# Forty short dummy matmuls instead of ten long ones at the head of an attention-and-experts kernel

## The chip, the cores and the metric

The kernel runs on one core of one Trainium2 chip. The metric is the device time of one execution in microseconds. The kernel before takes 563.89 us, the median of three runs (562.78 to 564.74).

TensorE (PE in the profile) multiplies matrices; VectorE (DVE), ScalarE (ACT) and GpSimd (POOL) do the elementwise work; SyncE (SP) issues nearly all DMAs. Each engine takes its instructions in the order in which the program lists them.

## The reference

```python
# sparse causal attention, B, H, S, D = 2, 8, 576, 64
scores = scale * np.matmul(q, k.transpose(0, 1, 3, 2))
mask_local = (rel >= 0) & (rel < 32)                     # heads 0 to 3
mask_strided = (rel >= 0) & (pos_k % 32 == pos_q % 32)   # heads 4 to 7
attn = softmax(np.where(masks, scores, -1e9))
x = np.matmul(attn, v)                                   # tokens 1152 x 512
# first layer, weights in float64
h = np.maximum(np.maximum(x @ w1, x @ w2), x @ w3)       # 512 -> 768
x = h @ w_out                                            # 768 -> 512
# four experts, all of them for every token
p = domain_probs / (domain_probs.sum(-1, keepdims=True) + 1e-09)
for e in range(4):
    out += p[:, e:e+1] * (np.maximum(x @ w1[e], 0) @ w2[e])   # 512 -> 1024 -> 512
```

## The kernel before

The 1152 tokens are worked on in four parts i (two batches, each in halves of 256 and 320 tokens), and the heads in four pairs p. The head of the program issues loads and then ten dummy matmuls: a tile `warm` is set to zero on VectorE (line 219), and line 222 multiplies it with itself into a PSUM bank that nobody reads. Their sole effect is that TensorE is at work while the first inputs are on their way.

Attention of a part and a pair has these steps. `att_a` (lines 280 to 339) puts the mask `mk` into a PSUM tile `sps` by a matmul with the identity (L306), adds the scores by float32 matmuls (L309), takes the maximum of each row on VectorE (L314), subtracts it in one of three ways (L325 on TensorE, L328 on VectorE, or as the bias of the exponential, L318 and L322) and takes the exponential on ScalarE (L322, L331, L334) into `p`. `att_n` divides by the sum: the reciprocal on VectorE (L355), the product on GpSimd (L361). `att_t` transposes `p` on TensorE (`tps`, L373) and ScalarE copies it to SBUF (`pt`, L376). `att_p` multiplies by the values (`ops`, L403); ScalarE and VectorE write the result as a pair of float16 tiles, high and low part, into `x` (L410, L411).

The first layer's weights come as float64 in six pieces `w_0` to `w_5` of 1.5 MB each into two staging buffers `st64_0` and `st64_1`. `decode64` makes float32 of them on VectorE, ScalarE and GpSimd (L198 to L214; the result for all six is one buffer `r`), `scale_w` finds a scale (a pass on ScalarE, L162; then small steps that end in the reciprocal `s`, L136), and `split_w` makes a high and a low float16 part (for `w_0` on GpSimd and ScalarE: L452, L453, L454). `g1` then multiplies `x` by the three matrices with three float16 matmuls for each product (L416 high by high, L417 high by low, L418 low by high). The second layer and the experts follow in the same float16 pairs.

In which order these steps are written is a table of names (`ORDER`). The order in which the instructions of each engine stand in the program is worked out from it when the program is built, by a scheduler that keeps a simulated timeline with costs of its own and, whenever an engine is free in it, takes the foremost step that is ready there. A change of what an early instruction costs in that timeline can thus move instructions far behind it.

Each tile has few buffers, and a later step waits until the earlier one has let go: two PSUM banks for `sps` (three for another tag that the first pairs use as well), two for `tps`, one for `ops`, one buffer for `r`.

Of the kernel before, what the change touches and what calls it, by code (L numbers as in the profile page):

```python
# [8 lines left out]
F32 = mybir.dt.float32  # L9
F16 = mybir.dt.float16  # L10
BF16 = mybir.dt.bfloat16
I32 = mybir.dt.int32
U16 = mybir.dt.uint16
AF = mybir.ActivationFunctionType
ALU = mybir.AluOpType
# [3 lines left out]
B, H, S, D = 2, 8, 576, 64  # L19
NT, DM, DFF = 1152, 512, 768  # L20
E, FE = 4, 1024
QN = (256, 320)

ATT = (((4, 64, 96, 288, 64), (4, 64, 64, 256, 64)), ((5, 64, 96, 352, 64), (6, 60, 108, 648, 108)))
NEG = -8.0e9
NWARM = 10
SUB = 'ddoppdpppoooodod'
ACC = 'bgbbgggggbggbggg'
SGN = 'dddpppdp'
# [30 lines left out]
TW = 'dddddddd'  # L60
TLO = 'd'
WHI = 'aaapaa'
TINY = 2.0**-100
REBIAS = 2.0**-112
TINY64 = 1.625 * 2.0**-124
# [3 lines left out]
def kernel(ctx, tc, qk0l, qk0s, qk1l, qk1s, vl, vs0, vs1, vn, masks, w123, wo, probs, we1, we2, out):  # L69
    nc = tc.nc  # L70
# [5 lines left out]
    x2acc = x2tp.tile([128, 4 * NT], F32, name="x2acc")  # L76
    x2j = [
        x2acc[:, 8 * QN[0] * j : 8 * (QN[0] + QN[1] * j)].rearrange("p (k b t) -> p k b t", k=4, b=2) for j in range(2)
    ]
# [14 lines left out]
    tp = moe_stack.enter_context(tc.tile_pool(name="tp", bufs=3))  # L94
# [21 lines left out]
    def nm(p):  # L116
        uid[0] += 1
        return f"{p}{uid[0]}"
# [20 lines left out]
    def scale_of(maxes, n, inv=None, f=0.25):  # L139

        allr, m = all_max(maxes, n)
        nc.vector.tensor_scalar(m, allr, TINY, f, ALU.max, ALU.mult)
        if inv is None:
# [45 lines left out]
    def decode64(g):  # L189
        hw, lw, r = groups[g]  # L190
        if not f64:
            return

        t = st64[g % 2]
        gi = hw.bitcast(I32)
        if LOW[g] == "a":
            top = t.bitcast(U16).rearrange("p (n t) -> p n t", t=4)[:, :, 1]
            nc.scalar.activation(lw, top, AF.Copy, bias=2.0**-14 - 0.5, scale=2.0**-13)  # L198
        else:
            nc.vector.tensor_scalar(lw, lw, 29, None, ALU.logical_shift_right)  # L200
        if SGN[g] == "d":
            nc.vector.scalar_tensor_tensor(lw, gi, -0x80000000, lw, ALU.bitwise_and, ALU.bitwise_or)
        else:
            sign = t.bitcast(BF16).rearrange("p (n t) -> p n t", t=4)[:, :, 1]
            nc.gpsimd.tensor_scalar(sign, hw, 0.0, 1.0, ALU.mult, ALU.mult)
        if REB[g] == "a":
            nc.scalar.activation(hw, hw, AF.Copy, scale=REBIAS)
        elif REB[g] == "p":
            nc.gpsimd.tensor_scalar(hw, hw, REBIAS, 1.0, ALU.mult, ALU.mult)
        else:  # L210
            nc.vector.tensor_scalar(hw, hw, REBIAS, None, ALU.mult)
        r = rp.tile([128, NP], F32, tag="r", name=nm("r")) if g < NF1 else hw
        gi, ri = hw.bitcast(I32), r.bitcast(I32)
        nc.vector.scalar_tensor_tensor(ri, gi, 3, lw, ALU.logical_shift_left, ALU.bitwise_or)  # L214
        groups[g][2] = r


    warm = tp.tile([128, 320], F32, tag="t1", name="warm")[:, :256].bitcast(BF16)
    nc.vector.memset(warm, 0.0)
    wps = ps.tile([128, 512], F32, tag="mm", name="wps")  # L220
    for _ in range(NWARM):
        nc.tensor.matmul(wps, warm[:, :128], warm, start=True, stop=True)

    tab = const.tile([128, 1], F32, name="tab")
    nc.scalar.activation(tab, warm[:, :1], AF.Exp)
# [2 lines left out]
    identb = const.tile([128, 128], BF16, name="identb")  # L228
# [14 lines left out]

    xs = [xp.tile([128, 4, 2, QN[i % 2]], F16, tag="x", name=f"x{i}") for i in range(4)]
    vinv = [None] * 4
    vsc = [None] * 4
    loaded = {}
# [32 lines left out]
    def att_a(i, p):  # L280
        hf = i % 2
        loc = p < 2
        t = loaded[i, p]
        ng, w, nk, kcols, kstep = ATT[hf][0 if loc else 1]
        rows = 2 * w
# [57 lines left out]
    def att_n(i, p):  # L343
        ng, w, nk, kcols, kstep = ATT[i % 2][0 if p < 2 else 1]
        rows = 2 * w
# [17 lines left out]
    def att_t(i, p):  # L363
        ng, w, nk, kcols, kstep = ATT[i % 2][0 if p < 2 else 1]
        rows = 2 * w
# [15 lines left out]
    def att_p(i, p):  # L381
        hf = i % 2
        loc = p < 2
        ng, w, nk, kcols, kstep = ATT[hf][0 if loc else 1]
        rows = 2 * w
        vt = loaded[i, "v", 0 if loc else 1]
        ov = psa.tile([128, 512], F32, tag="o", bufs=1, name=nm("ops"))
        for c0, n, ptt in pts_of[i, p]:
            for j in range(n):
                g = c0 + j  # L390
                for a in range(2):
                    rhs = ptt[:nk, j * rows + a * w : j * rows + a * w + w]
                    col = 128 * (p % 2) + 64 * a
                    lhsT = vt[:, g, col : col + 64]
                    if loc:
                        o = ov[64 * a : 64 * a + 64, 64 * g : 64 * g + 64]
                    else:
                        nr = (8, 6)[hf]
                        o = ov[64 * a : 64 * a + 64, : w * ng].rearrange("p (m c) -> p m c", c=nr * ng)[
                            :, :, nr * g : nr * g + nr  # L400
                        ]
                        rhs = rhs.rearrange("p (m r) -> p m r", r=nr)
                    nc.tensor.matmul(o, lhsT, rhs, start=True, stop=True)  # L403
        if loc:
            src = ov[:, : 64 * ng]
            dst = [xs[i][:, p, j, :] for j in range(2)]
        else:
            src = ov[:, : w * ng].rearrange("p (m c) -> p m c", c=(8, 6)[hf] * ng)[:, :, :32]
            dst = [xs[i][:, p, j, :].rearrange("p (m r) -> p m r", r=32) for j in range(2)]
        nc.scalar.activation(dst[0], src, AF.Copy, scale=vsc[i])  # L410
        nc.vector.scalar_tensor_tensor(dst[1], src, vsc[i], dst[0], ALU.mult, ALU.subtract)  # L411

    def mm3(psum, pairs):
        n = len(pairs)
# [27 lines left out]
    def split_w(fc):  # L442
        hi, lo = [ws[fc][j].rearrange("p w k f -> p (w k f)") for j in range(2)]
        r = groups[fc][2]
        if WLO[fc] == "d":
            if WHI[fc] == "a":
                nc.scalar.activation(hi, r, AF.Copy, scale=wsc[fc])
# [10 lines left out]
    def g1(i, fc):  # L458
        n = QN[i % 2]
        if fc == 0:  # L460
# [20 lines left out]
    def g2(i, dc):  # L481
        n = QN[i % 2]
        x2 = x2j[i % 2][:, dc, i // 2, :]
# [52 lines left out]
    def x2_ops(j, pool):  # L536
        n = QN[j]
        s, xinv[j] = scale_of(x2mx[:, j::2, :], 8, f=2.0)
# [106 lines left out]
    def gemm1(e, j, fp):  # L645
        ops = wx[e, 1][0]
        n = QN[j]
        hh = hbuf[0] if j else hbuf[1 + e % 2]
# [120 lines left out]
    def first_hidden():  # L769
        if "m" not in gens:  # L770
            open_h0()
            gens["m"] = stream((fp, lambda fp=fp: gemm1(0, 0, fp)) for fp in range(4))
        next(gens["m"])

    ATOMS = {
        "cl": open_rest,
        "m": lambda: first_hidden(),
        "yw": lambda: gen_step("x1", lambda: x2_ops(1, lay["left"])),
        "lq": load_qk, "lv": load_v, "lw": load_w, "lo": load_wo,
# [8 lines left out]
    for a in ORDER.split():  # L788
        name = a.rstrip("0123456789")
# [212 lines left out]
def _layout(inputs):  # L1002
# [102 lines left out]
```

## Time and profile before

| what | value |
|---|---|
| median of three runs | 563.89 us |
| the profiled execution | 563.27 us |
| its span, first to last instruction | 561.5 us |
| TensorE busy | 544.6 us (97%) |
| VectorE, ScalarE, GpSimd busy | 410.6, 345.4, 101.0 us |
| mean granted clock of TensorE | 0.978 |

The span is 1.8 us shorter than the time of the execution it belongs to. Busy time of TensorE says that it had a matmul in flight, not that it ran at its peak. The granted clock is a share of full speed: 1.00 is 2.4 GHz and 0.50 is 1.2 GHz. In the 40 slices of the page the clock is below 0.9 in the first three slices alone, that is in the first 42 us.

### The profile page before, as it was taken

To read this page: it belongs to the slowest core of one execution; us is meant where nothing else is said; L and a number is where in the kernel's file an instruction comes from. 1 tells how busy PE (TensorE), PEld (TensorE's weight loads), DVE (VectorE), ACT (ScalarE), POOL (GpSimd) and SP (SyncE) were. 2 spreads that over 40 slices of the span, in tenths; PEclk is the share of its full clock that TensorE was granted. 3 is DMA by queue.
4 is the path that set the end of the run, shared out by engine and by line. 5 is a ranking of instruction groups with operands and counts; after the bars stand their busy time and mean duration, and the time that the engine had idled before them with its cause. 6 is when DMAs were issued, how large, how long until landed. Compare 5 with 4: busy or idle time off the path is not lost.

```text
span 561.5 us, 11622 instructions
## 1 busy us (share of the span) xinstructions
PE 544.6 (97%) x4681; PEld 450.3 (80%) x4681; DVE 410.6 (73%) x794; ACT 345.4 (62%) x794; POOL 101.0 (18%) x82
## 2 busy tenths in 40 slices
PE   7899999999999999999999999999889999999997
PEld 4678788888877778778888877888767888877886
DVE  3979989662459424779564789898888999878832
ACT  3588676655245255999876877347887544777200
POOL 0465871710112103000000300000130000120000
PEclk7679999999999999999999999999999999999999
DMA  8999633024004000204516001544501321101332
GB/s 311 336 410 277 189 121 114 2 76 152 1 5 148 1 0 1 76 20 152 188 66 198 2 1 40 150 149 142 161 1 39 118 90 57 40 1 31 130 104 75
DMA packets 24150, 58.60 MB, mean 104 GB/s; under 512 B 3272, under 2 KB 3528, under 8 KB 23328
## 3 DMA queue, kind: packets, MB, share of 16 engines
q1 hardware_dynamic: 23952, 57.57, 31.4%
q8 instruction: 36, 0.59, 0.5%
q10 hardware_dynamic: 144, 0.30, 0.1%
q14 instruction: 18, 0.15, 0.1%
HBM read 48.42 MB, written 9.44 MB: 103 GB/s over the span
## 4 chain that ended last, share of the span: by engine, by line
PE 84%; DMA 6%; DVE 4%; ACT 4%; POOL 1%; issue 0%; SPq 0%; DVEq 0%; ACTq 0%
PE e L827 15%; PE w L827 13%; PE g L416 9%; PE g L417 9%; PE g L418 8%; PE e L659 4%; PE e L660 4%; PE e L661 4%; PE w L659 4%; PE w L661 4%; PE w L660 4%; PE ops L403 2%; DMA st<-in_w_dram 2%; PE sps L309 2%; DMA mk<-in_masks_dram 1%; PE tps L373 1%
## 5 line engine op out<-in xcount | busy, mean ns | idle before, releaser
L827 PEld LDWEIGHTS <-hb 128*128 128x128 f16 x1056 | 103.1, 98 | 12.6
L418 PE MATMUL g<-x,w 128*128 128x256 f16 (+1 forms) x288 | 82.0, 287 | 0.0
L417 PE MATMUL g<-x,w 128*128 128x256 f16 (+1 forms) x288 | 82.0, 287 | 0.0
L416 PE MATMUL g<-x,w 128*128 128x256 f16 (+1 forms) x288 | 80.8, 287 | 1.0 <-ACT x L410 0.6
L659 PE MATMUL e<-xops,w1ops 128*128 128x320 f16 (+1 forms) x224 | 63.7, 288 | 2.9 <-ACT c L670 1.5
L660 PE MATMUL e<-xops,w1ops 128*128 128x320 f16 (+1 forms) x224 | 64.2, 288 | 0.0
L659 PE MATMUL w<-xops,w1ops 128*128 128x256 f16 (+1 forms) x224 | 63.4, 284 | 0.8 <-DVE c L687 0.6
L661 PE MATMUL e<-xops,w1ops 128*128 128x320 f16 (+1 forms) x224 | 64.1, 288 | 0.0
L660 PE MATMUL w<-xops,w1ops 128*128 128x256 f16 (+1 forms) x224 | 63.4, 284 | 0.0
L661 PE MATMUL w<-xops,w1ops 128*128 128x256 f16 (+1 forms) x224 | 62.9, 284 | 0.0
L660 PEld LDWEIGHTS <-w1ops 128*128 128x128 f16 x448 | 43.8, 98 | 15.0 <-issue 4.7
L661 PEld LDWEIGHTS <-w1ops 128*128 128x128 f16 x448 | 43.8, 98 | 11.0
L659 PEld LDWEIGHTS <-w1ops 128*128 128x128 f16 x448 | 43.8, 98 | 10.3
L417 PEld LDWEIGHTS <-w 128*128 128x128 f16 x288 | 28.2, 98 | 8.1 <-issue 1.1
L416 PEld LDWEIGHTS <-w 128*128 128x128 f16 x288 | 28.2, 98 | 8.0 <-issue 0.8
L418 PEld LDWEIGHTS <-w 128*128 128x128 f16 x288 | 28.3, 98 | 7.4 <-issue 0.2
L476 POOL TENSOR_TENSOR h<-t,h 128x320 f16<-128x320 f32 (+1 forms) x18 | 16.4, 916 | 88.2 <-ACT h L475 88.2
L162 ACT ACTIVATE junk<-st 128x512 f16<-128x512 f32 x44 | 27.8, 631 | 5.6 <-DMA st<-in_we_dram 4.7
L827 PE MATMUL w<-B,hb 128*128 128x256 f16 x240 | 29.4, 273 | 0.0
L169 ACT ACTIVATE w1ops<-st,s 128x1024 f16<-128x1024 f32 x19 | 21.4, 1144 | 12.9 <-DVE st L584 4.8
L827 PE MATMUL e<-B,hb 128*128 128x256 f16 x240 | 29.1, 273 | 0.0
L714 POOL TENSOR_TENSOR hb<-c,hb 128x512 f16<-128x512 f32 x7 | 9.0, 1279 | 108.7 <-ACT hb L713 99.8
(232 smaller groups left out, 1318.4 us busy)
## 6 DMA issues: line engine op xcount, KB each, us to landing
st<-in_we_dram SPq DMA_DIRECT2D x10, 1024.0 KB, 5.3
st<-in_w_dram SPq DMA_DIRECT2D x6, 1536.0 KB, 9.7
c<-accd SPq DMA_DIRECT2D x24, 256.0 KB, 2.8
accd<-c SPq DMA_DIRECT2D x23, 256.0 KB, 2.3
st<-in_wo_dram SPq DMA_DIRECT2D x2, 1536.0 KB, 6.4
st<-in_we_dram SPq DMA_DIRECT2D x6, 512.0 KB, 4.6
x2acc<-in_we_dram SPq DMA_DIRECT2D x6, 512.0 KB, 4.3
qk<-in_qk1s_dram SPq DMA_DIRECT2D x4, 684.0 KB, 11.8
```

Of the source, the lines that this page charges most:

```text
L162: nc.scalar.activation(junk, src, AF.Abs, scale=2.0**-12, accum_out=dst)
L169: nc.scalar.activation(hi, src, AF.Copy, scale=s)
L309: nc.tensor.matmul(s3[:, j, :], qv[:, g, :], t[:, kstep * g : kstep * g + nk], start=False, stop=j == n - 1)
L403: nc.tensor.matmul(o, lhsT, rhs, start=True, stop=True)
L416: nc.tensor.matmul(psum, lh, rh, start=i == 0, stop=False)
L417: nc.tensor.matmul(psum, lh, rl, start=False, stop=False)
L418: nc.tensor.matmul(psum, ll, rh, start=False, stop=i == n - 1)
L476: eng(HLO[6 * i + fc]).tensor_tensor(hh[:, 1, fc, :], t1[:, :n], hh[:, 0, fc, :], ALU.subtract)
L659: nc.tensor.matmul(pt, wh, xh, start=first and k == 0, stop=False, skip_group_check=True)
L660: nc.tensor.matmul(pt, wh, xl, start=False, stop=False, skip_group_check=True)
L661: nc.tensor.matmul(pt, wl, xh, start=False, stop=k == 1, skip_group_check=True)
L827: nc.tensor.matmul(pt, hop[:, x, f, sl], wop[:, y, f, :], start=start and n == 0, stop=stop and n == 11, skip_group_check=True)
```

## The change

The dummy matmuls are forty of 256 columns instead of ten of 512. Their operand is the head of `x2acc`, a large tile that is written by real work only much later, instead of a tile of its own. Nothing else that the program executes is altered by hand: the matmuls of `att_p` now start a PSUM group at the first block alone (`start=g == 0`), and the remaining lines add options (`XLO`, a value "a" of `SGN`, an atom "z" of `ORDER`) that no table uses here. Line numbers rise by 1 to 4 in `decode64`, by 8 in `att_a` to `att_t` and by 15 in `g1` (L200 becomes L201, L202 L206, L211 L215, L214 L218, L306 L314, L309 L317, L325 L333, L361 L369, L162 L163, L416 L431).

```diff
-NWARM = 10
+NWARM = 40
...
-    warm = tp.tile([128, 320], F32, tag="t1", name="warm")[:, :256].bitcast(BF16)
+    warm = x2acc[:, :128].bitcast(BF16)
     nc.vector.memset(warm, 0.0)
     wps = ps.tile([128, 512], F32, tag="mm", name="wps")
-    for _ in range(NWARM):
-        nc.tensor.matmul(wps, warm[:, :128], warm, start=True, stop=True)
+
+    def keep_warm(n):
+        for _ in range(n):
+            nc.tensor.matmul(wps[:, :256], warm[:, :128], warm, start=True, stop=True)
+
+    keep_warm(NWARM)
...
-                    nc.tensor.matmul(o, lhsT, rhs, start=True, stop=True)
+                    nc.tensor.matmul(o, lhsT, rhs, start=g == 0, stop=True, skip_group_check=True)
```

The scheduler places the instructions of attention and of the first layer's first parts anew on every engine, up to the part of 320 columns; behind that the order is the old one. Numbers in the names below are those of the tiles: `p11` and `p61` are the same tiles before and after, only the last number differs.

On VectorE, about 20 us into the program, `s30` is the scale of the weight piece `w_0`, and `st64_1` the staging buffer of `w_1`. Before:

```order
L131 TENSOR_REDUCE rows42_276<-rows42_276 128x1
L145 TENSOR_SCALAR sinv_134<-rows29_230 128x1
L200 TENSOR_SCALAR st64_1_72<-st64_1_72 128x1536
L142 TENSOR_SCALAR rows42_276<-rows42_276 128x1
L338 TENSOR_REDUCE asm25_210<-p23_208 128x4
L136 RECIPROCAL s30_235<-sinv_134 128x1
L202 SCALAR_TENSOR_TENSOR st64_1_72<-st64_1_72 128x1536
```

Now:

```order
L146 TENSOR_SCALAR sinv_163<-rows29_259 128x1
L132 TENSOR_REDUCE rows42_305<-rows42_305 128x1
L137 RECIPROCAL s30_264<-sinv_163 128x1
L143 TENSOR_SCALAR rows42_305<-rows42_305 128x1
L346 TENSOR_REDUCE asm25_239<-p23_237 128x4
L201 TENSOR_SCALAR st64_1_72<-st64_1_72 128x1536
L146 TENSOR_SCALAR inv43_309<-rows42_305 128x1
```

The scale of `w_0` now stands ahead of the first decoding step of `w_1` (L200 before, L201 now).

On GpSimd, `r27` and `w123_0` are the two steps that split `w_0`; `p35`, `p23` and `p11` are three products of `att_n`. Before:

```order
L452 TENSOR_SCALAR r27_226<-r27_226,s30_235 128x1536
L361 TENSOR_TENSOR p35_253<-p35_253,ar49_296 128x384
L454 TENSOR_TENSOR w123_0_142<-r27_226,w123_0_142 128x1536
L361 TENSOR_TENSOR p23_208<-p23_208,ar56_318 128x256
L361 TENSOR_TENSOR p11_171<-p11_171,ar58_323 128x384
```

Now:

```order
L467 TENSOR_SCALAR r27_255<-r27_255,s30_264 128x1536
L469 TENSOR_TENSOR w123_0_171<-r27_255,w123_0_171 128x1536
L369 TENSOR_TENSOR p35_282<-p35_282,ar49_325 128x384
L369 TENSOR_TENSOR p23_237<-p23_237,ar56_347 128x256
L369 TENSOR_TENSOR p11_200<-p11_200,ar58_352 128x384
```

The low part of `w_0` has moved ahead of `p35`, and `p11` is now the third product behind it, not the second.

On ScalarE, `p61` is an exponential that frees a bank of `sps`, and `w123_1` with `mx89` the pass over the decoded `w_1` (`r34`). Before:

```order
L322 ACTIVATE p61_339,asm63_341<-sps64_342,amx62_340 128x64 x4
L349 ACTIVATE ars72_377<-asm63_341 128x4
L410 ACTIVATE x0_130<-ops112_520,s44_282 128x256
L198 ACTIVATE st64_0_71<-st64_0_71 128x1536
L162 ACTIVATE w123_1_222,mx89_444<-r34_251 128x1536
L376 COPY pt66_359<-tps65_354 96x512
L322 ACTIVATE p75_386,asm77_388<-sps78_389,amx76_387 128x64 x4
```

Now:

```order
L418 ACTIVATE x0_159<-ops112_549,s44_311 128x256
L163 ACTIVATE w123_1_251,mx89_473<-r34_280 128x1536
L330 ACTIVATE p61_368,asm63_370<-sps64_371,amx62_369 128x64 x4
L199 ACTIVATE st64_0_71<-st64_0_71 128x1536
L384 COPY pt66_388<-tps65_383 96x512
L330 ACTIVATE p75_415,asm77_417<-sps78_418,amx76_416 128x64 x4
L384 COPY pt68_395<-tps67_390 64x512
```

The exponential `p61` stood two places ahead of the copy of `x0`; it now stands behind the pass over `w_1`.

On VectorE at the same place, `sps82` and `sps87` are tiles of scores whose maxima are taken, and `st64_0` holds the weight piece `w_2`. Before:

```order
L202 SCALAR_TENSOR_TENSOR st64_0_71<-st64_0_71 128x1536
L314 TENSOR_REDUCE sps82_404<-sps82_404 128x4
L211 TENSOR_SCALAR st64_0_71<-st64_0_71 128x1536
L318 TENSOR_SCALAR amx80_402<-sps82_404 128x4
L314 TENSOR_REDUCE amx85_422<-sps87_424 120x3
```

Now:

```order
L322 TENSOR_REDUCE sps82_433<-sps82_433 128x4
L206 SCALAR_TENSOR_TENSOR st64_0_71<-st64_0_71 128x1536
L326 TENSOR_SCALAR amx80_431<-sps82_433 128x4
L215 TENSOR_SCALAR st64_0_71<-st64_0_71 128x1536
L363 RECIPROCAL ar73_408<-ars72_406 128x4
L322 TENSOR_REDUCE amx85_451<-sps87_453 120x3
```

Two decoding steps of `w_2` (L202 and L211 before, L206 and L215 now) stood on either side of the maximum of `sps82`; both now stand between it and the maximum of `sps87`.

## Rows read from the trace of the kernel before

**Rows 1.** Busy time (instructions) of PE, PEld, DVE, ACT, POOL; granted clock; DMA share, GB/s.
```profile
40.00:60.00 20.00, 20.00 (x193) 17.03 (x192) 18.42 (x40) 16.58 (x65) 12.02 (x8) 1.00 0.79 235
```

**Rows 2.** Timeline, start to 16 us: start, duration, engine, line, work [idle before].
```profile
1.19 4.09 PE L222 MATMUL wps<-warm 128*128 128x512 bf16 x10 [1.19 <-DVE vm L272]
...
4.58 0.71 PE L222 MATMUL wps<-warm 128*128 128x512 bf16 x2
8.28 1.23 PE L306 MATMUL sps<-mk,identb 128*128 128x256 bf16 x4 [3.00 <-DMA mk<-in_masks_dram]
9.30 6.92 PE L309 MATMUL sps<-qk 128*128 128x64 f32 x32
```

**Rows 3.** The same windows by 1 us, where the granted clock changes.
```profile
8.00:9.00 1.00, 0.72 (x3) 0.40 (x3) 0.00 (x0) 0.92 (x1) 0.00 (x0) 0.60 1.04 417
...
25.00:26.00 1.00, 0.94 (x7) 0.52 (x7) 1.00 (x6) 0.12 (x1) 0.84 (x1) 0.64 1.17 480
...
35.00:36.00 1.00, 1.00 (x8) 0.76 (x6) 1.00 (x2) 0.46 (x3) 1.00 (x1) 0.74 1.02 421
```

**Rows 4.** Timeline of VectorE, 21 to 37 us.
```profile
21.08 1.23 DVE L200 TENSOR_SCALAR st<-st 128x1536 int32<-128x1536 int32 x1 [0.34 <-DMA st<-in_w_dram]
...
22.63 0.15 DVE L136 RECIPROCAL s<-sinv 128x1 f32<-128x1 f32 x1
...
31.37 2.16 DVE L214 SCALAR_TENSOR_TENSOR r<-st 128x1536 int32<-128x1536 int32 x1 [1.26 <-POOL w L454]
...
33.91 1.92 DVE L202 SCALAR_TENSOR_TENSOR st<-st 128x1536 int32<-128x1536 int32 x1
35.75 0.55 DVE L314 TENSOR_REDUCE sps<-sps 128x4 f32<-128x384 f32 x1
36.22 0.94 DVE L211 TENSOR_SCALAR st<-st 128x1536 f32<-128x1536 f32 x1
```

**Rows 5.** GpSimd: its timeline, then groups by form in 20 to 21.6 and 33 to 34.7 us.
```profile
27.54 3.80 POOL L454 TENSOR_TENSOR w<-r,w 128x1536 f16<-128x1536 f32 x1
...
L361 POOL TENSOR_TENSOR p<-p,ar 128x384 f32<-128x384 f32 x1 | 0.8, 827 | 0.0
L361 POOL TENSOR_TENSOR p<-p,ar 128x256 f32<-128x256 f32 x1 | 0.6, 614 | 18.8 <-DVE ar L355 18.8
...
L361 POOL TENSOR_TENSOR p<-p,ar 128x384 f32<-128x384 f32 x1 | 2.3, 2337 | 0.0
```

**Rows 6.** Timeline of ScalarE, 29 to 35 us.
```profile
29.48 0.31 ACT L322 ACTIVATE p<-sps,amx 128x64 f32<-128x64 f32 x1
...
30.56 0.21 ACT L322 ACTIVATION_READ_ACCUMULATOR p<-sps,amx 128x1 f32 x1
...
31.85 1.63 ACT L198 ACTIVATE st<-st 128x1536 int32<-128x1536 uint16 x1
33.56 1.49 ACT L162 ACTIVATE w<-r 128x1536 f16<-128x1536 f32 x1
```

**Rows 7.** Timeline of TensorE (PEld loads its weights), 25 to 40 us.
```profile
25.82 1.78 PEld L309 LDWEIGHTS sps<-qk 128*128 128x128 f32 x8 [0.48 <-DMA qk<-in_qk0s_dram]
...
29.58 0.80 PE L416 MATMUL g<-x,w 128*128 128x256 f16 x3 [0.57 <-ACT x L410]
...
31.36 0.82 PE L417 MATMUL g<-x,w 128*128 128x256 f16 x3
...
32.94 1.86 PE L309 MATMUL sps<-qk 128*128 128x96 f32 x8
34.59 1.49 PE L373 MATMUL tps<-ident,p 128*96 128x128 f32 x8
...
36.89 0.69 PE L403 MATMUL ops<-pt,v 96*64 96x64 f32 x16
...
39.06 0.81 PE L325 MATMUL sps<-amx,ident 120*120 120x324 f32 x2 [0.29 <-DVE amx L314]
```

**Rows 8.** TensorE's waits from 20 us on: total us, times, longest.
```profile
PE ops L403 <- DVE x L411: 0.9, 1, 0.9
```

More of the change, by code (lines that the diff above doesn't have):

```diff
@@ L21 @@
 E, FE = 4, 1024
-QN = (256, 320)
-ATT = (((4, 64, 96, 288, 64), (4, 64, 64, 256, 64)), ((5, 64, 96, 352, 64), (6, 60, 108, 648, 108)))
-NEG = -8.0e9
-NWARM = 10
+QN = [256, 320]
+ATT = [[[4, 64, 96, 288, 64], [4, 64, 64, 256, 64]], [[5, 64, 96, 352, 64], [6, 60, 108, 648, 108]]]
+NEG = -8000000000.0
+NWARM = 40
 SUB = 'ddoppdpppoooodod'
@@ L62 @@
 WHI = 'aaapaa'
+XLO = 'dddddddddddddddd'
 TINY = 2.0**-100
@@ L200, in decode64 @@
             nc.vector.tensor_scalar(lw, lw, 29, None, ALU.logical_shift_right)
-        if SGN[g] == "d":
+        if SGN[g] == "a":
+            sign = t.bitcast(F16).rearrange("p (n t) -> p n t", t=4)[:, :, 1]
+            nc.scalar.activation(sign, hw, AF.Copy, scale=2.0**-60)
+        elif SGN[g] == "d":
             nc.vector.scalar_tensor_tensor(lw, gi, -0x80000000, lw, ALU.bitwise_and, ALU.bitwise_or)
@@ L410, in att_p @@
         nc.scalar.activation(dst[0], src, AF.Copy, scale=vsc[i])
-        nc.vector.scalar_tensor_tensor(dst[1], src, vsc[i], dst[0], ALU.mult, ALU.subtract)
+        if XLO[4 * i + p] == "e":
+            if (i, "n") not in loaded:
+                loaded[i, "n"] = x2acc[:, 4096 + 64 * i : 4160 + 64 * i].bitcast(BF16)
+                nc.vector.tensor_scalar(loaded[i, "n"], identb, vinv[i], -1.0, ALU.mult, ALU.mult)
+            nc.tensor.matmul(src, loaded[i, "n"], dst[0], start=False, stop=True, skip_group_check=True)
+            nc.scalar.activation(dst[1], src, AF.Copy, scale=vsc[i])
+        else:
+            nc.vector.scalar_tensor_tensor(dst[1], src, vsc[i], dst[0], ALU.mult, ALU.subtract)
     def mm3(psum, pairs):
@@ L776 @@
         "cl": open_rest,
+        "z": keep_warm,
         "m": lambda: first_hidden(),
```

## The prediction

> **What bounds the kernel now.** I read the busy shares by stage first, then the head of the timeline, the clock, and last the three engines that feed TensorE in the first 40 us. From 40 us on TensorE is busy without a gap at the full clock [rows 1]; the end is the moment from which it runs full plus a fixed amount of work. So the change is worth what it moves before that moment, and what it adds in waits behind it.
>
> The head shows what the change aims at. Ten dummies take 4.09 us from 1.19 on; the last two take 0.71, where the average says 0.82, so the clock came up at their end. Then TensorE stands idle for 3.00 us until the mask lands, does the four mask matmuls, and takes 6.92 us for the first 32 passes of scores [rows 2]. At 8 to 9 us the granted clock falls towards 0.50, the lower of the two levels. It falls again in 25 to 26 us and comes back for good in 35 to 36 us [rows 3].
>
> But at the head TensorE is not what the others wait for. The chain that matters runs over VectorE: the scale of weight piece w_0 is ready at 22.78 us, held up behind a decoding step of w_1 that had itself waited 0.34 us for its DMA [rows 4]; GpSimd makes the low part of w_0 from 27.54 to 31.34 us [rows 5]; TensorE has its first product of the layer at 29.58 and the products with the low part of w_0 at 31.36 [rows 7]. Only from there on is TensorE the bound, and until 35.5 us at the low clock.
>
> **The dummies.** Forty matmuls of 256 columns take 0.21 us each at the low clock (half of 4.09 / 10, an estimate) and about 0.11 at the high one (half again). With the clock up some 3.6 us after the start, as before, 17 run low and 23 high: 3.6 + 2.5 = 6.1 us, from about 1.1 to 7.2 us. Bounds: all high 4.4 us, end at 5.5; all low 8.5 us, end at 9.6. The mask is there at 8.28 [rows 2]. I take 7.2, so the idle time shrinks from 3.0 to about 1 us. The first 32 passes then run at the high clock and may halve, but VectorE has no use for them sooner: it works without a gap on its own list. Value on the end: 0, since VectorE covers it. The operand tile and the group flags cost nothing: no wait hangs on them, and the flags leave the order as it was.
>
> **w_0 sooner: a gain that is hidden.** The scale s30 now stands ahead of L201. In the rows it stood behind that step's 0.34 us of idle time and its 1.23 us, and two small steps of 0.3 us together: 1.9 us [rows 4]. The low part of w_0 loses the product p35 ahead of it on GpSimd too, but p35 had run while ScalarE made the high part, so the shift stays about 2.0: from 31.34 to 29.3 us. Does TensorE use it? Its first product needs x0, and x0 needs ops60, which stands behind scores whose data landed at 25.82 and which then take 1.8 us [rows 7]. The DMA is the same, so the first product stays at about 29.5, and behind it come ops112 with 1 us of TensorE. The six products with the low part start at about 31.3, where they started before. Gain 0; if the clock is high here, those scores and ops60 shrink by half and up to 1.3 us are gained. I take 0.
>
> **p11 and the transposes.** Behind those six (to 32.8 us) TensorE now has tps65, which needs p11, the third GpSimd product behind w_0's low part. Before, scores (sps82) stood between, and tps65 came at 34.59 [rows 7]. Alone, such products take 0.83 us (384 wide) and 0.61 (256 wide); the p11 of before took 2.34, beside VectorE's L214 (31.37 to 33.53) [rows 4, 5]. In the new order L218 and p35 are let go by the same event, the end of w_0's low part. I take p35 first, then L218 as long as that takes alone, 1.75 (2.16 less the 0.4 us it now waited out behind a product), then p23 and p11: 29.3 + 0.83 + 1.75 + 0.61 + 0.83 = 33.3 us. TensorE waits 0.5 us. Bounds: without any contention 31.6 and no wait; with all three as slow as the 2.34 row, 36.3 and 3.5 us.
>
> The Trainium skill states why (SBUF — State Buffer, "SBUF: two separate sides"): VectorE with two SBUF inputs and GpSimd share a port pair under an exclusive lock, and the loser "fully blocks". The 2.34 row agrees: it is the 0.83 of its shape plus most of the time of L214. By a pool of shared bandwidth the three products would only be stretched, and p11 would come between 31.6 and 33.3.
>
> **p61 and the scores behind it.** The two transposes take 1.49 us [rows 7]: 34.8. The scores sps82 need the bank that p61 reads. p61 now stands behind the pass over w_1, which needs r34 (L218, done at about 31.9): 31.9 + 1.7 (L162 and its read-out) + 1.3 (p61, 29.48 to 30.77) = 34.9 [rows 6]. That is just hidden behind p11. Behind it on ScalarE stand the decoding of w_2, 1.63 [rows 6], and the copy pt66 at about 37.0, on which ops117 waits. On TensorE sps82 takes 1.9 and tps70 0.7: 37.5. ops117 started at 36.89 before [rows 7], with the same work done ahead of it. Late by 0.6; by 1.0 at its end if the clock is still low. I take 0.8.
>
> **The maximum of sps87.** VectorE now has both decoding steps of w_2 between the maxima of sps82 and sps87. sps82 is done at 36.8; its maximum 0.55, the decoding 1.92 and 0.94, small steps 0.2, the maximum of sps87 0.5 [rows 4]: 40.9 less overlaps of 0.2, so 40.7. L325 (now L333) of sps87 started at 39.06 [rows 7]. It now starts 1.7 later, but three products (0.33 us), which stood behind it, stand ahead of it now: late by 1.4 in all. From there on I see TensorE full, with the same work left. Bounds of this term together with the one before: 0, if p11 and the clock come early, and 2.8, if VectorE gets no overlap and TensorE stays low.
>
> **Sum.** 0 + 0 + 0.8 + 0.6 = 1.4 us later. Of that a little may vanish in the 0.9 us for which TensorE waited for VectorE later on [rows 8]; I leave it in. The profiled execution took 563.27 us (span 561.5 and 1.8 around it): 564.7. The median of the runs lies 0.6 above that execution: 565.3 us.
>
> A difference below 0.3% (1.7 us) can't be told from no change in this kernel. My forecast thus lies in "no change", on its slow side; its own range is 564.2 to 566.8.
>
> **Rivals.** *Absorbed* (564.0): p11 comes unhindered at 31.6 and VectorE keeps its slack, so that TensorE is full from the same time as before. For it: the chains of w_0 and r34 are 2 us earlier. Against it: the order on VectorE.
>
> *Warm through* (561.5): the clock, once up, stays up to 35 us. On TensorE's own list from 27.9 to 35.5 us it would halve some 6 us of work, of which GpSimd and VectorE give back less than 3; with the first product 1.3 us sooner I take 2.4. Against it: in 22 to 25 us the clock was up, TensorE had two waits of about a us, and it fell [rows 3]; between the first scores and the release by VectorE the new order still leaves TensorE idle. The Trainium skill (TensorE: Matmul & The Clock Gate, "Why this matters for your kernels") would have the clock kept by leaving no long gap between bursts, which speaks for this rival at the mask and against it after the first scores.
>
> *Cold for longer* (568.0): the clock came up in 35 to 36 us after a stretch without a wait: products, sps82, two blocks of transposes. The new order puts waits for p11 and for the maximum of sps87 into that stretch. If it comes up later by as long as that stretch took (32.6 to 35.5, some 3 us), TensorE does about 3 us at half the speed: 1.5 us more, and VectorE's next maxima are late by as much again, about 1.2 us of it seen: 565.3 + 1.5 + 1.2. It decides if those waits come before the clock does.
>
> *Dummies outlast the mask* (566.5): the clock stays low through all forty, they end at 9.6 us, the first scores are 1.3 us late, and VectorE's first maximum with them; its list then moves by about 1.2. Against it: the last two dummies of before were already faster.
>
> **How the numbers follow.** Forecast 0.37 (of it 0.07 above 1.7 us), absorbed 0.19, warm through 0.18 (all but 0.02 faster by over 0.3%), cold for longer 0.21, outlasting 0.05 (slower). Faster 0.16; slower 0.07 + 0.21 + 0.05 = 0.33, and 0.02 for an unnamed new wait later on, 0.35; no change 0.49. For 8 in 10 the range reaches from inside the warm case to the cold one: 562.0 to 568.2.
>
> **What would show it.** The dummies end before the mask's landing, idle time ahead of the first mask matmul about 1 us, the 32 passes in 4 us or less. w_0's low part at about 29.3. A wait of tps65 for GpSimd, ops117 at 37 to 38 us, the wait of L333 for VectorE longer than 0.29 us. The forecast is wrong if TensorE is full earlier than before, if the clock is high between 26 and 35 us, or if the difference arises behind 60 us.

## The result and the profile after

| | before | after |
|---|---|---|
| median of six runs | 563.99 us (562.78 to 564.85) | 570.9 us (568.93 to 573.38) |
| the profiled execution, its span | 563.27, 561.5 us | 568.93, 567.1 us |

The change makes the kernel slower: ratio 1.0123, 95% interval [1.0103, 1.0144]. The forecast of 565.3 us was wrong, and its range (to 568.2) misses the time. The profiled execution of after is the fastest of its six runs, so its rows show 5.6 us of the loss, not all 7.

The head is what the change promised. The timeline of TensorE (start, duration, line, work, [idle before]) answers to [rows 2]: the dummies reach the mask, no idle time is left ahead of it, and the first scores run fast, only to wait for data instead. The last row is TensorE's first product of the first layer: it comes at 27.39 us, 29.58 before.

```profile
1.05 7.06 PE L228 MATMUL wps<-x2acc 128*128 128x256 bf16 x40 [1.05 <-DVE vm L280]
8.01 0.70 PE L314 MATMUL sps<-mk,identb 128*128 128x256 bf16 x4
8.79 1.10 PE L317 MATMUL sps<-qk 128*128 128x64 f32 x8
10.45 1.13 PE L317 MATMUL sps<-qk 128*128 128x96 f32 x8 [0.56 <-DMA qk<-in_qk0l_dram]
12.43 3.10 PE L317 MATMUL sps<-qk 128*128 128x96 f32 x16 [0.85 <-DMA qk<-in_qk0l_dram]
...
27.39 0.49 PE L431 MATMUL g<-x,w 128*128 128x256 f16 x3 [0.57 <-ACT x L418]
```

The clock (windows of 1 us as in [rows 3]; the third number from the end) reads high until 13 us, then falls; it is high once more from 23 us on, falls again at 30 us, behind 2.16 us in which TensorE stood still, and is back for good at 37 us, about 1.5 us later than before.

```profile
13.00:14.00 1.00, 1.00 (x8) 1.00 (x7) 1.00 (x2) 0.59 (x3) 0.00 (x0) 0.54 1.11 396
...
30.00:31.00 1.00, 0.96 (x16) 0.87 (x16) 1.00 (x1) 0.00 (x0) 1.00 (x2) 0.57 0.97 393
...
37.00:38.00 1.00, 1.00 (x20) 0.75 (x18) 1.00 (x2) 1.00 (x7) 0.00 (x0) 1.00 0.95 403
```

The scale of w_0 and its low part are there early, as forecast (VectorE and GpSimd; [rows 4, 5]), but beside the low part VectorE's L215, 0.94 us in [rows 4], takes 2.73 (the same step of w_1 took 1.35 before), and x0's low part, queued behind it, is ready no sooner than before.

```profile
20.10 0.15 DVE L137 RECIPROCAL s<-sinv 128x1 f32<-128x1 f32 x1
...
26.34 2.73 DVE L215 TENSOR_SCALAR st<-st 128x1536 f32<-128x1536 f32 x1
...
29.52 0.47 DVE L426 SCALAR_TENSOR_TENSOR x<-ops,s,x 128x256 f16<-128x256 f32 x1
```
```profile
25.16 3.10 POOL L469 TENSOR_TENSOR w<-r,w 128x1536 f16<-128x1536 f32 x1 [2.08 <-ACT w L468]
28.21 4.41 POOL L369 TENSOR_TENSOR p<-p,ar 128x384 f32<-128x384 f32 x3
```

TensorE ([rows 7]) pays with 2.16 us, and the places that the forecast named follow:

```profile
30.04 1.06 PE L411 MATMUL ops<-pt,v 64*64 64x64 f32 x16 [2.16 <-DVE x L426]
31.03 0.40 PE L432 MATMUL g<-x,w 128*128 128x256 f16 x1
...
32.68 1.94 PE L381 MATMUL tps<-ident,p 128*96 128x128 f32 x8 [0.18 <-POOL p L369]
...
37.39 0.69 PE L411 MATMUL ops<-pt,v 96*64 96x64 f32 x16
...
40.74 0.81 PE L333 MATMUL sps<-amx,ident 120*120 120x324 f32 x2 [0.86 <-DVE amx L322]
```

But the loss goes on. Where TensorE was full in 40 to 60 us [rows 1], it now is not, and from 60 to 80 us it stands still for 4.06 us of 20; before (second fence) it was 1.74.

```profile
40.00:60.00 20.00, 18.47 (x175) 15.39 (x175) 18.58 (x45) 13.89 (x52) 10.61 (x8) 1.00 0.77 227
60.00:80.00 20.00, 15.94 (x167) 13.51 (x166) 17.66 (x25) 12.07 (x42) 19.14 (x9) 1.00 0.44 137
80.00:100.00 20.00, 18.96 (x195) 16.18 (x194) 18.26 (x37) 12.53 (x39) 5.99 (x6) 1.00 0.35 118
```
```profile
60.00:80.00 20.00, 18.26 (x201) 15.77 (x200) 19.15 (x33) 12.74 (x39) 18.03 (x8) 1.00 0.52 150
```

Of the waits of TensorE behind 41 us the three long ones are all for VectorE:

```profile
61.98 0.81 PE L333 MATMUL sps<-amx,ident 120*120 120x324 f32 x2 [1.18 <-DVE amx L322]
...
71.31 0.74 PE L381 MATMUL tps<-ident,p 128*96 128x128 f32 x5 [1.46 <-DVE inv L146]
...
78.85 0.27 PE L431 MATMUL g<-x,w 128*128 128x256 f16 x1 [1.29 <-DVE t L488]
```

A good ruler for two orders of the same work is an instruction that both have once per step: ScalarE's copy of the first product of each of the 24 blocks of the first layer. The blocks come in the same order in both. The last copy starts at 199.23 us before and at 205.47 after, 6.2 us late; between 41 and 100 us TensorE's idle time grew from 1.74 to 5.89 us, by 4.15 (0.79 us in 41 to 60 us and the rows above); so about 2.1 us were lost up to 41 us and twice as much behind it (TensorE has no idle time between 100 and 199 us in either). From there to the end 0.6 us comes back.

What VectorE does between 45 and 70 us, after:

```profile
47.24 1.74 DVE L166 TENSOR_REDUCE mx<-st 128x1 bf16<-128x1536 f32 x1
48.90 2.71 DVE L218 SCALAR_TENSOR_TENSOR r<-st 128x1536 int32<-128x1536 int32 x1
...
59.27 1.13 DVE L201 TENSOR_SCALAR st<-st 128x1536 int32<-128x1536 int32 x1
60.31 1.21 DVE L491 TENSOR_TENSOR h<-t,h 128x256 f16<-128x256 f32 x1
61.44 0.48 DVE L322 TENSOR_REDUCE amx<-sps 120x3 f32<-120x324 f32 x1
61.85 2.42 DVE L465 SCALAR_TENSOR_TENSOR w<-r,s,w 128x1536 f16<-128x1536 f32 x1
...
64.78 4.33 DVE L218 SCALAR_TENSOR_TENSOR r<-st 128x1536 int32<-128x1536 int32 x1
```

and before:

```profile
44.97 1.75 DVE L214 SCALAR_TENSOR_TENSOR r<-st 128x1536 int32<-128x1536 int32 x1
...
53.66 0.49 DVE L314 TENSOR_REDUCE amx<-sps 120x3 f32<-120x324 f32 x1 [0.45 <-PE sps L309]
...
56.18 1.81 DVE L450 SCALAR_TENSOR_TENSOR w<-r,s,w 128x1536 f16<-128x1536 f32 x1
...
58.90 1.75 DVE L214 SCALAR_TENSOR_TENSOR r<-st 128x1536 int32<-128x1536 int32 x1
```

The reader is to see three things. The maximum over w_3 (L166) stands ahead of L218 of w_2 now. L201 of w_4 and a low part of h (L491) now stand ahead of the maximum of a block of scores (L322; L314 at 53.66 us before), for which TensorE waits at 62 us, and ahead of the splitting of w_2 (L465), which comes 5.7 us late. And L218, 1.75 us before, takes 2.71 and 4.33 beside GpSimd's signs of w_3 and w_4:

```profile
46.50 3.78 POOL L209 TENSOR_SCALAR st<-st 128x1536 bf16<-128x1536 f32 x1 [2.48 <-ACT st L199]
...
62.62 5.14 POOL L209 TENSOR_SCALAR st<-st 128x1536 bf16<-128x1536 f32 x1
```

L218 frees a staging buffer, so the loads of w_4 and w_5 go out at 51.67 and 69.17 us, against 46.79 and 60.72 before.

### The profile page after: what moved, and what is told of

Same layout as the page of the kernel before. It is cut to its first block, busy times and chain, and to the rows that moved or that the text cites. A ratio compares the mean times of both kernels' runs of the same rounds, so it can differ in the third digit from the quotient of the medians.

```text
span 567.1 us, 11680 instructions
## 1 busy us (share of the span) xinstructions
PE 546.3 (96%) x4711; PEld 451.0 (80%) x4711; DVE 413.9 (73%) x794; ACT 345.0 (61%) x794; POOL 101.9 (18%) x82
## 4 chain that ended last, share of the span: by engine, by line
PE 76%; DVE 9%; DMA 8%; ACT 6%; issue 2%; SPq 0%; DVEq 0%; ACTq 0%
PE e L843 14%; PE w L843 12%; PE g L431 8%; PE g L432 8%; PE g L433 8%; PE e L674 4%; PE e L676 4%; PE e L675 4%; PE w L674 4%; PE w L676 4%; PE w L675 4%; DMA v<-in_vl_dram 2%; DMA st<-in_we_dram 2%; DMA v<-in_vs_dram 2%; DVE r L218 2%
## 5 line engine op out<-in xcount | busy, mean ns | idle before, releaser
L431 PE MATMUL g<-x,w 128*128 128x256 f16 (+1 forms) x288 | 80.4, 286 | 2.7 <-DVE t L488 1.5
L431 PEld LDWEIGHTS <-w 128*128 128x128 f16 x288 | 28.2, 98 | 8.2 <-issue 1.0
L163 ACT ACTIVATE junk<-st 128x512 f16<-128x512 f32 x44 | 27.8, 631 | 6.1 <-DMA st<-in_we_dram 5.2
L491 POOL TENSOR_TENSOR h<-t,h 128x320 f16<-128x320 f32 (+1 forms) x18 | 15.9, 885 | 80.2 <-ACT h L490 80.2
```

What stands on the lines that cost most here:

```text
L163: nc.scalar.activation(junk, src, AF.Abs, scale=2.0**-12, accum_out=dst)
L431: nc.tensor.matmul(psum, lh, rh, start=i == 0, stop=False)
L491: eng(HLO[6 * i + fc]).tensor_tensor(hh[:, 1, fc, :], t1[:, :n], hh[:, 0, fc, :], ALU.subtract)
```

## The experiments

All kernels are edits of after, or of it with the ten dummies of 512 columns. Three theories were set against each other: the new order of the instructions (A), the longer head with its clock (B), and the short form of the dummies or another part of the edit (C). Medians stand beside the median of before in the same comparison, ratios with their 95% interval.

| run | order | us (before) | ratio |
|---|---|---|---|
| n0: no dummies | old | 563.28 (563.59) | 0.9994 [0.9979, 1.0009] |
| c512_10: ten of 512 | old | 563.76 (563.59) | 1.0002 [0.9986, 1.0018] |
| n20: 20 of 256 | old | 566.37 (563.81) | 1.0032 [1.0007, 1.0056] |
| c64_80: 80 of 64 | old | 565.88 (563.81) | 1.0048 [1.0026, 1.0070] |
| n24: 24 of 256 | new | 570.58 (563.81) | 1.0109 [1.0088, 1.0129] |
| n44: 44 of 256 | a third | 568.53 (563.59) | 1.0086 [1.0062, 1.0111] |
| n56: 56 of 256 | a fourth | 568.57 (563.59) | 1.0080 [1.0050, 1.0111] |

**Order or head.** With 0 and 20 dummies of 256 columns, as with ten of 512, the scheduler gives the old order, with 24 the one of 40. So 20 and 24 part the theories A and B.

```diff
-NWARM = 40
+NWARM = 20        # n20; 24 in n24, 44 in n44, 56 in n56, 0 in n0
```

> The kernel after with 20 dummies of 256 columns in place of 40: 5120 columns as before the change, but in the short form, on the new operand tile and with the new group flags. Every engine's instructions stand in the order of before. Theory A (the loss comes from the new order of the instructions): 564 us, as before. Theory B (the loss comes from the longer run of dummies at the head, by the clock that it sets or by the time it takes): 564 us too. Theory C (the short form, the operand tile or the group flags cost something by themselves): up to 571 us.

> The kernel after with 24 dummies of 256 columns: 6144 columns, only 1024 more than before, so the head is nearly that of before (dummies ending near 5.5 us, over 2 us idle until the mask lands). Every engine's instructions stand in the order of after. Theory A (order): 570 to 571 us, as after, with L218 of the third and fourth weight piece again beside GpSimd's decoding. Theory B (head): 564 to 565 us.

Four dummies more, 4.2 us more between the medians. The head of n24 is nearly that of before (first fence), yet its wait at 62 us is the one of after, with the same length. Its clock comes back in 35 to 36 us (last row), as in [rows 3]:

```profile
1.05 4.60 PE L228 MATMUL wps<-x2acc 128*128 128x256 bf16 x24 [1.05 <-DVE vm L280]
8.27 1.01 PE L314 MATMUL sps<-mk,identb 128*128 128x256 bf16 x3 [2.62 <-DMA mk<-in_masks_dram]
...
62.44 0.81 PE L333 MATMUL sps<-amx,ident 120*120 120x324 f32 x2 [1.18 <-DVE amx L322]
```
```profile
35.00:36.00 1.00, 0.83 (x5) 0.58 (x4) 0.00 (x0) 1.00 (x8) 0.00 (x0) 0.74 1.02 419
```

So the new order is the larger part of the loss, and the length of the dummies is no part that these runs can tell: 24 and 40 cost the same within the intervals. n20 also lost 0.3% in the old order (2.6 us between the medians), which A did not expect; every kernel with a new order has short dummies too, so the share of the order alone is the step from n20 to n24, 4.2 us of the 6.8 that n24 loses.

```diff
-NWARM = 40                                   # c64_80
+NWARM = 80
-            nc.tensor.matmul(wps[:, :256], warm[:, :128], warm, start=True, stop=True)
+            nc.tensor.matmul(wps[:, :64], warm[:, :128], warm[:, :64], start=True, stop=True)
```

> The kernel after with 80 dummies of 64 columns: again 5120 columns, so the order of before is kept, but every dummy loads its 128 weight columns, so that on the chip the run should last well beyond the 4 us of before, to some 7 or 8 us (or longer). It separates head and order: a long head with the old order. Theory A (order): 564 us; a long head in the old order gives 563 to 565. Theory B (head): 570 to 571 us. If the dummies outlast the mask at about 8 us by x, up to x more.

This missed its aim: the 80 dummies took 4.45 us, not 7 or 8, so no long head was tried in the old order. It repeats n20: short dummies, old order, half a per cent. Theory C is thus not ruled out for the rest of the loss; n20 and c64_80 were timed in one comparison and the next two runs in another, so it is open whether the short form or the comparison makes the difference.

```diff
-    warm = x2acc[:, :128].bitcast(BF16)       # c512_10
+    warm = x2acc[:, :256].bitcast(BF16)
-            nc.tensor.matmul(wps[:, :256], ...
+            nc.tensor.matmul(wps, ...         # with NWARM = 10
```

> The kernel after with the dummies of before: ten of 512 columns; the operand stays at the head of x2acc and the group flags of att_p stay. The instructions stand in the order of before on every engine. It does those two edits alone. Theory A (order): 564 us, as before. Rival D (one of the two edits lengthens the program or makes it vary more, as the kernel with 20 dummies of 256 columns suggests with 566.4 and runs from 562.6 to 569.3): 566 us, runs spread over 5 us or more.

> The kernel after without any dummy matmul; order of before on every other instruction. TensorE is idle until the mask lands and starts cold. Theory A with slack at the head (VectorE and GpSimd set the pace up to 31 us, whatever TensorE's clock): 564 to 565 us. Theory B (the clock at the head is worth something): the first 32 passes of scores run wholly at the low clock, VectorE's first maxima come 1 to 2 us later: 565.5 to 567 us.

The operand tile and the group flags are worth nothing, as forecast. And no dummies at all are as good as ten: without them the first 32 passes take 7.25 us, 6.92 in [rows 2], and the end does not move. So the head has slack in the old order, and the ten dummies were worth nothing at the end.

```profile
8.37 1.23 PE L314 MATMUL sps<-mk,identb 128*128 128x256 bf16 x4 [8.37 <-DMA mk<-in_masks_dram]
9.38 7.25 PE L317 MATMUL sps<-qk 128*128 128x64 f32 x32
```

> The kernel after with 44 dummies of 256 columns: 0.45 us more at the head, and a third order of the instructions in which the splitting of w_2 (L465) and the last decoding step of w_3 (L218) stand 8 to 9 places later still on VectorE. Theory A (order): a time of its own, that follows when L218 of w_3 ends and w_5 can be loaded (61 us before, 69 after); with those places 570 to 575 us. Theory B (head): the dummies now end at 8.5 us, half a us past the mask: 571 to 571.5.

> The kernel after with 56 dummies of 256 columns: they end near 9.8 us, some 1.8 us past the mask, and the scheduler gives a fourth order, in which the splitting of w_2 stands right behind L201 of w_4 as in after, and L218 of w_3 one place sooner. Theory A (order): its own time, by when L218 of w_3 ends: 566 to 571 us. Theory B (head: a later first score costs what it is late): 571 + 1.8 = 573 us.

Two more orders, both slower than before. By the medians neither is so slow as after, though their heads are longer, but the intervals overlap. In n56 the dummies end at 10.06 us, 2 us past the time at which the mask is there in the other runs; what that alone costs can't be told, since the order is another too. For n44 the forecast by places in VectorE's list (570 to 575) missed: a later splitting of w_2 did not make it worse.

**GpSimd beside VectorE.** In the order of after, work was taken off GpSimd where it stands beside stretched steps of VectorE; the order stays the same on every engine.

```diff
-            nc.gpsimd.tensor_tensor(lo, r, hi, ALU.subtract)
+            k = 192 if fc == 0 else NP        # lo0part, a_slo
+            nc.gpsimd.tensor_tensor(lo[:, :k], r[:, :k], hi[:, :k], ALU.subtract)
-            nc.gpsimd.tensor_scalar(sign, hw, 0.0, 1.0, ALU.mult, ALU.mult)
+            k = {3: 192, 4: 1216}.get(g, NP)  # a_s, a_slo; {3: 192} in b_s
+            nc.gpsimd.tensor_scalar(sign[:, :k], hw[:, :k], 0.0, 1.0, ALU.mult, ALU.mult)
```

> The kernel after, but GpSimd makes only an eighth of the low part of w_0 (192 of 1536 columns; the rest is left out, so its output is not the reference's). Order of after on every engine. It takes away the contention of that step (3.1 us) with VectorE's L215 (2.73 us against 0.95 elsewhere) and so, by theory A1 (the loss begins there), the 2.16 us wait of TensorE for x0's low part: L215 in about 1 us, the products with the low part sooner, 1.5 to 2.5 us of the 7 us gone: 568 to 569 us. Rival A2 (the head of the layer has slack, the loss arises behind 45 us, from the weight pieces on VectorE beside GpSimd's decoding and the loads queued behind them): 570 to 571 us, with the waits behind 50 us unchanged.

> The kernel after, order unchanged on every engine, but GpSimd sets the signs in only 192 of 1536 columns of the weight piece w_3 and in 1216 of w_4 (the rest is left out, so its output is not the reference's). In after these two steps take 3.78 and 5.14 us and VectorE's L218 beside them 2.71 and 4.33 us instead of 1.75. Theory E (what the new order costs behind 45 us is VectorE stretched beside GpSimd): L218 of w_2 1.75 to 1.9 us, L218 of w_3 about 3, w_5's load at 67 us instead of 69.2, TensorE's wait at 62 us at most 0.3 instead of 1.18, in all 568 to 569 us. Rival F (the new order costs by its dependences alone, contention has slack): 570 to 571 us.

> The kernel before this one in the list, with GpSimd making an eighth of the low part of w_0 as well: all three places where GpSimd stretches VectorE in the new order are relieved, the order is that of after. Theory E: the gains add, since the 2 us won up to 40 us no longer come back as a wait at 62 us: 566 to 567.5 us. Rival F: as with the low part of w_0 alone, 569 us.

> Control: the order of before (dummies ten of 512 columns), with GpSimd setting the signs in only 192 of 1536 columns of w_3 (the rest is left out). In before that step took 3.67 us and stood beside VectorE's steps without stretching L214 (1.75 us). Theory E: hardly anything to win, 563 to 564 us. Rival F: 563.8 us. If leaving the work out is itself worth a us or more whatever the order, it shows here: 562.5 us or less.

Measured: lo0part 569.03 (1.0078 [1.0059, 1.0097]), a_s 570.48 (1.0101 [1.0072, 1.0130]), a_slo 568.52 (1.0077 [1.0048, 1.0105]), b_s 564.67 (1.0009 [0.9990, 1.0027]). In lo0part L215 took 0.94 us and TensorE was ahead of after by 2 us at 40 us, but most of it was eaten at 62 us, where its wait grew from 1.18 to 2.74. The steps of VectorE (second fence) show why: L201, which now stands ahead of the maximum, waits for the load of w_4, and the splitting of w_2, 1.81 us before, takes 4.50 beside GpSimd's signs of w_4.

```profile
61.93 0.81 PE L333 MATMUL sps<-amx,ident 120*120 120x324 f32 x2 [2.74 <-DVE amx L322]
```
```profile
58.75 1.32 DVE L201 TENSOR_SCALAR st<-st 128x1536 int32<-128x1536 int32 x1 [0.67 <-DMA st<-in_w_dram]
...
61.80 4.50 DVE L465 SCALAR_TENSOR_TENSOR w<-r,s,w 128x1536 f16<-128x1536 f32 x1
```

What is left is 1.5 us between the medians of n24 and lo0part, whose intervals overlap a little. In a_s L218 of w_2 came down to 1.77 us and that of w_3 to 3.61, TensorE's wait at 62 us stayed at 1.18, and the time did not move clear of noise. So the forecast of theory E (568 to 569) missed, but it is not refuted: one of the two stretches was only partly gone, and the profiled execution, the slowest of its six, was 3.3 us behind that of after at the step that is L333 at 40.74 us above (44.06) and 2.3 at the end, so it had made up 1 us between. a_slo is no faster than lo0part either; there the splitting of w_2 still takes 3.76 us. b_s shows that leaving out the signs of w_3 is worth nothing by itself in the old order.

```diff
             nc.vector.scalar_tensor_tensor(lo, r, wsc[fc], hi, ALU.mult, ALU.subtract)
+            if fc == 2:                       # inject, on c512_10
+                nc.gpsimd.tensor_scalar(x2acc[:, 1024:2560], lo, 1.0, 1.0, ALU.mult, ALU.mult)
```

> The order of before (dummies ten of 512 columns), with one GpSimd step added that computes nothing: it reads the low part of w_2 and writes 1536 float32 columns of x2acc that nobody reads, so it is let go by the same event as L218 of w_3 (58.6 us) and runs beside it. Theory E: L218 of w_3 takes 3 to 4 us instead of 1.75, w_5's load goes out 1.3 to 2.3 us later, and since VectorE is full there, TensorE waits for it later on: 564.7 to 566 us. Rival F: VectorE has the slack to take it in, 563.5 to 564.2 us.

566.26 against 564.34 (1.0040 [1.0022, 1.0058]): one useless GpSimd step of 1.47 us costs the old order 2 us. L218 took 2.46 us, and TensorE waited 3.15 us at 65 us (0.90 before). Of these 2.25 us more, about 1 us is VectorE's: its L426 there ends 0.96 us later than before, of which L218's stretch is 0.71. For the rest TensorE had come to this place 1.3 us sooner in this execution. So VectorE has no slack there to take in even 0.7 us. GpSimd's own next step came 0.96 us later as well, so the 2 us need not all go by VectorE.

```profile
58.55 1.47 POOL L467 TENSOR_SCALAR x2acc<-w 128x1536 f32<-128x1536 f16 x1 [2.87 <-DVE red L127]
```
```profile
65.45 1.12 PE L411 MATMUL ops<-pt,v 64*64 64x64 f32 x16 [3.15 <-DVE x L426]
```

**Single steps of VectorE put back.** Steps of after were issued behind another step of VectorE, as in the old order. The scheduler then shifts other instructions behind them too. In dve_old and dve_old_lo one name of `ORDER` (`vs1`) is moved as well, and the kernels with `_lo` cut the low part of w_0 as in lo0part.

```diff
-            nc.vector.tensor_scalar(lw, lw, 29, None, ALU.logical_shift_right)
+            with tc.issue_after(lay["r3"]) if g == 4 else ExitStack():   # r3: L218 of w_3
+                nc.vector.tensor_scalar(lw, lw, 29, None, ALU.logical_shift_right)
...
+            with tc.issue_after(lay["a13"]) ...   # dve_old alone: the maximum over v, and
+        with tc.issue_after(lay["r3"]) ...        # the low part of h of block (0, 1)
...
+            with tc.issue_after(lay["r", 2]) if fc == 3 else ExitStack():  # mx_later
+                absmax(mx, groups[fc][0])
```

> The kernel after with one step of VectorE moved: L201 of w_4, which waits for a load of 1.5 MB, is issued behind L218 of w_3 as in the order of before, and not ahead of the maximum of the scores at 61.4 us and of the splitting of w_2. Up to there VectorE's list is the same otherwise. Theory G (what VectorE has in front of those two decides): both come 1.1 us sooner, TensorE's wait of 1.18 us at 62 us goes, 569.5 us; more only if the steps behind it follow. Rival F (any order but the old one costs, by many small waits): 570 to 571 us.

> The kernel before this one in the list, with GpSimd making only an eighth of the low part of w_0 (the rest is left out). In the order of after that alone gave 2 us at 40 us, of which the wait at 62 us took back most (1.18 to 2.74 us; 569.0 in all), because L201 waited for its load. Theory G: without L201 in front the 2 us stay: 567 to 567.5 us. Rival F: 569 us as before.

> The kernel after with three steps of VectorE issued later, as in the order of before: L201 of w_4 and the low part of h (L491) behind L218 of w_3, and the maximum over a value tile (1.73 us) behind the maximum of the last block of scores of that part. The splitting of w_2 moves up by 8 places, to where the old order had it. The head keeps its 40 dummies and the new order up to 45 us. Theory G: the splitting of w_2 some 3 to 4 us sooner (57 to 58.5 us instead of 61.85), L218 of w_3 near 61, w_5's load near 63 instead of 69.2; of the 7 us 3 to 4 are gone, 566 to 568 us. Rival F: 569 to 571 us.

> The kernel before this one in the list, with GpSimd making only an eighth of the low part of w_0 (the rest is left out): both places relieved, in the order of dve_old. Theory G: the time of before or nearly so, 563.5 to 565.5 us. Rival F: not under 567 us.

> The kernel after with one swap on VectorE taken back: the maximum over w_3 (L166, 1.74 us) is issued behind L218 of w_2, as in the order of before, and not ahead of it. Theory W (the loss behind 41 us hangs on when the staging buffers come free): L218 of w_2 at 47.2 us beside GpSimd's decoding only at its end (1.8 to 2.7 us), w_4's load at 49 to 49.8 us instead of 51.7, w_5's and both loads of the output weights 1 to 2.5 us sooner, 568.5 to 569.5 us. Rival F (many small waits, no chain): 570 to 571 us.

> The same, and L201 of w_4 issued behind L218 of w_3 too (alone that gave 568.0 us against 562.8 of before, and w_5's load at 66.0 us instead of 69.2). Theory W: w_4's load at 49 to 49.8 us, w_5's at 63 to 65, the last load near 92, and the time follows it: 565.5 to 567 us. Rival F: 568 us or more.

| run | us (before) | ratio | loads of w_4, w_5, last |
|---|---|---|---|
| later201 | 568.0 (562.82) | 1.0093 [1.0063, 1.0123] | 51.8, 66.0, 94.3 us |
| later201_lo | 567.16 (562.82) | 1.0061 [1.0037, 1.0085] | 52.4, 66.6, 94.9 |
| dve_old | 572.63 (562.82) | 1.0166 [1.0143, 1.0189] | 51.1, 64.6, 95.8 |
| dve_old_lo | 572.28 (562.82) | 1.0170 [1.0135, 1.0204] | 50.3, 63.9, 94.5 |
| mx_later | 571.38 (563.49) | 1.0154 [1.0124, 1.0183] | 52.1, 71.1, 98.3 |
| mx_201_later | 573.24 (563.49) | 1.0175 [1.0147, 1.0202] | 51.3, 67.9, 96.2 |

L201 alone gained a little, not separated from after by the intervals; the wait at 62 us is gone in it. With GpSimd's low part of w_0 cut as well, a third to a half of the loss is gone (4.3 us left between the medians). All three of theory G's steps together made it slower, though the splitting of w_2 came at 58.46 us, as expected: G is refuted. mx_later shows best why such a repair fails. L218, put ahead of the maximum over w_3, now stands wholly beside GpSimd's sign step and takes 4.36 us; w_4's load is no sooner, and the maximum, moved behind it, makes TensorE wait:

```profile
47.62 4.36 DVE L218 SCALAR_TENSOR_TENSOR r<-st 128x1536 int32<-128x1536 int32 x1
51.91 1.74 DVE L166 TENSOR_REDUCE mx<-st 128x1 bf16<-128x1536 f32 x1
```
```profile
46.90 3.76 POOL L209 TENSOR_SCALAR st<-st 128x1536 bf16<-128x1536 f32 x1 [2.49 <-ACT st L199]
```
```profile
53.71 0.23 PE L130 MATMUL rows<-identb,mx 128*128 128x128 bf16 x1 [1.63 <-DVE mx L166]
```

That the swap helps by freeing the buffer sooner (theory W) thus could not be tried: it did not free it sooner. In the profiled runs w_4's load goes out at 45.5 to 48.4 us in every kernel with the old order, and at 48.9 to 55.6 in every other. This goes with the loss but was not shown to cause it, and among the new orders it does not: by the medians n44, with the latest load of w_4 (55.6), loses less than after, and dve_old_lo, which loads w_4 and w_5 sooner than after (50.3 and 63.9), loses more. What stays open: which steps of the new order make up the part behind 41 us, and why short dummies cost the old order 0.3 to 0.5%. The profiled run of n20 lost 1.0 us against that of c512_10 up to 200 us and had 1.4 us of idle time behind 300 us that the other had not; one run of each tells no more. No kernel tried beats before.

## Why the prediction was wrong

- **The dummies, value 0 on the end.** Right for their number: none against ten in the old order, and 24 against 40 in the new one, give no difference. For their short form it is not shown, since n20 and c64_80 lost 2.6 and 2.1 us in the old order. They took 7.06 us, not 6.1 (by the two paces of the forecast some 26 of them ran slow, not 17), and ended with the mask. The first 32 passes took 6.7 us (8.79 to 15.5), not 4 or less: TensorE waited twice for data, and the clock fell at 13 us.
- **w_0 sooner, gain 0.** The low part came at 28.26 us (forecast 29.3), and the six products with it still started at 31.03. The gain of 0 was right for another reason than the one given: I held scores and ops60 for the cause, but with the clock high from 23 us on the first product came 2.1 us sooner than forecast, and then x0's low part waited behind L215, stretched by 1.8 us. That the time came out the same is luck. lo0part, with the stretch gone, is 1.5 us faster than n24, so there was something to gain.
- **p11 and p61.** Waits of 0.18 and 0.16 us where 0.5 and a hidden one were forecast; ops117 at 37.39 (forecast 37.5), L333 at 40.74 (forecast 40.7), behind both decoding steps of w_2 as forecast: here the mechanism held. By the reckoning of the forecast that is the 1.4 us; by the copies and the idle time above it was about 2.1.
- **The step that failed: "From there on I see TensorE full, with the same work left."** Between 41 and 100 us TensorE stood still for 4.15 us more than before, and 3.9 of its 5.9 us of idle time there are the three waits for VectorE above. I took TensorE's full row of 40 to 60 us for slack on the others. But VectorE was busy for 18.42 of those 20 us [rows 1], so its list had little room for a new order, and the `inject` run bears it out: 1.47 us put beside it cost 2 us. The step from n20 to n24 shows that the new order costs 4.2 us; which of its moved steps make up which part is argued from the rows, not shown. The forecast had gone through the changed list of VectorE only as far as the maximum of sps87. It named its own test, a difference that arises behind 60 us, and most of it did; "an unnamed new wait later on" had been given a chance of 0.02.
- **Rivals.** "Cold for longer" came nearest in size, by another mechanism: the clock came back about 1.5 us later, but n24, where it came back as early as before, lost as much. "Warm through" failed: the clock fell at 13 us, with no gap on TensorE since the first dummy longer than 0.85 us, so that leaving no long gap did not keep it, and again at 30 us; the 2.2 us by which the first product came sooner went into the wait of 2.16. "Dummies outlast the mask" did not come true: they ended as the mask came.

## What to carry to other kernels

When an edit at the head makes a scheduler place instructions anew, separate the two at once: look for the smallest step of the edit that keeps the old order and the smallest that gives the new one, and time both. Follow the changed order of the second-busiest engine to where the order is the old one again; while TensorE shows no gap, its next inputs can still hang on another engine that has no slack. Putting single steps back did not bring the old time back here, since the others stood elsewhere by then.

## What the runs showed of the hardware

VectorE's L218, with two inputs of 1536 int32 columns, takes 1.75 us alone and 4.36 when it starts 0.7 us behind a GpSimd step of 3.76 us: 2.6 of the 3.0 us that both had left were lost to it, and GpSimd lost nothing. The Trainium skill says so (SBUF — State Buffer, "SBUF: two separate sides": the loser "fully blocks"), and these rows agree but for the last 0.4 us. A reduction over as many columns (L166, 1.74 us) beside the same step of GpSimd kept its time. In after, where L465 was at it first, GpSimd's sign step itself took 5.14 us instead of 3.8; in lo0part the same sign step started first, at 61.16 us, and took 3.79, and L465, 0.6 us behind it, took 4.50 instead of 1.81. So either engine can lose, and here the later one did. The loser can be small: in n24 it is a step of 4 columns, 0.15 us alone, that stood beside nearly all of the low part of w_0.

```profile
25.32 3.06 DVE L361 TENSOR_SCALAR ars<-asm 128x4 f32<-128x4 f32 x1
```
```profile
25.24 3.11 POOL L469 TENSOR_TENSOR w<-r,w 128x1536 f16<-128x1536 f32 x1 [1.59 <-ACT w L468]
```
